# Copying every unit's V-product bank out in two column halves, on ScalarE and VectorE

## The chip, the cores and the metric

The kernel runs on one core of a Trainium2 chip. A core has a matrix engine (TensorE), three other compute engines (VectorE, ScalarE, GpSimd) and DMA queues that the sync engine and others feed. Every engine works through its own instructions in the order in which the program gives them, and waits on semaphores for the others. The metric is the device time of one execution, in microseconds; lower is better.

## The reference

The input x has 2048 rows (tokens) of 512 numbers. It is normalised by rows, and two branches are computed from it, attention with 32 heads of 16 numbers each and a gated MLP:

```
xn  = layernorm(x)
qkv = (xn @ wqkv)  -> q, k, v per head
p   = softmax(q @ k^T * 16 ** -0.5)
s   = (p @ v, heads side by side) @ wo
g   = silu(gelu(xn @ w1 + b1) @ w2 + b2)
out = x + s * g
```

All of it is in fp32. The attention is the part that the change touches.

## The kernel before, in words

The first part (to about 475 us) normalises x, makes q, k and v, runs the MLP and begins with the row maxima of the scores. The second part, the main loop of lines 954 to 972, is the attention, and the last part is the product with wo, the gate and the sum.

**Units and steps.** The attention is cut into 32 units: a group of 4 heads (8 groups) times a chunk of 512 queries (4 chunks). A unit `u` takes 16 steps, one for each block `k` of 128 keys; the loop's counter `n` is 16u + k. There are 512 steps and one more to finish.

**What a step does.** The string `ORDER[3]`, "TSXTTSTYV", gives the order of the work in a step for n from 2 to about 490:

- "T" (four times, `t_one`, line 702): one head's scores, keys along the partitions and 512 queries along the columns, as one product on TensorE (line 709) into a PSUM bank, and then the exponential of it by ScalarE (line 711) into a tile in SBUF. There are four banks for this, one (tile name `ps`) for the first T of a step and three (`pst`) in turn for the others. A T product waits until the exponential has read what was in its bank before.
- "S" (twice): scores of a later unit with queries along the partitions, as one product (line 178), and VectorE's maximum over the columns of it (line 184). They are needed for the softmax's shift.
- "X" and "Y": two half-wide products of the same kind in one bank, Y after X, and one maximum over both (line 184), recorded behind Y. So a step has three such reductions on VectorE.
- "V" (`pv_step`, line 768): the V product of the step before. Four matmuls on TensorE, one for each head, add `vsb` (the values, with a column of ones for the softmax's denominator) times the exponentials into one bank, the tile `pv`. The profile shows eight matmul records for it.

S, X and Y use three banks in a ring (`s_ring`): S takes the first and puts it at the end of the ring at once, X takes the next and Y puts that one back. By this order, the first S product of a step takes the bank of the first S of the step before, X takes that of the second S, and the second S takes that of X and Y. Each waits for VectorE's reduction of that bank.

In the last steps (n from about 491) there are no S, X and Y left; the order is "TTTTV", and the products with wo (line 880) run between.

**The end of a unit.** The pool `ps_v` has one bank, so the V products of all units go into the same one, one unit after the other. When the 16th V product of a unit is done (`k == NT - 1`), its result is copied from the bank to the tile `os` in SBUF (lines 777 to 784). The copy stands behind that V product in the program. ScalarE has the four exponentials of that step in front of it and those of the next step behind it; on VectorE, what stands in front of the place is the reduction of Y, and the next step's reductions follow. The first V product of the next unit comes at the end of the next step, after its T, S, X and Y products, and waits until the bank has been copied out.

For units 0 to 30 the whole copy is one instruction on ScalarE (line 781). For the last unit, 31, the columns are halved: ScalarE copies the first 256 (line 783), VectorE the other 256 (line 784).

From `os` the DMA queue then moves the denominators (line 794) and the four heads' rows (line 797) to other tiles. The moves are issued by the sync engine one step later; nine steps after the copy, VectorE takes the reciprocals of the denominators (line 802), which go through DRAM into a tile that GpSimd multiplies with (line 811).

**The loop's other work.** At some steps VectorE reduces a unit's maxima (line 239) or transposes them (line 258). In the last steps ScalarE and VectorE compute the gates (lines 834, 835) and VectorE multiplies the results (line 890).

Of the kernel before, what the change touches and what calls it, by code (L numbers as in the profile page):

```python
# [10 lines left out]
AF = mybir.ActivationFunctionType  # L11
# [29 lines left out]
HC = CH // 2  # L41
# [6 lines left out]
def fused(ctx: ExitStack, tc: tile.TileContext, x, wqk, wv, wo, w1, b1, w2, b2, out):  # L48
    nc = tc.nc
# [37 lines left out]
    NU = NG * NCH  # L87
# [679 lines left out]
    PV, OS, DN, DR = {}, {}, {}, {}  # L767
    def pv_step(u, k):
        g = u // NCH
        if k == 0:  # L770
            PV[u] = ps_v.tile([P, CH], F32, name="pv")
        for j in range(GH):
            h, w = (g * GH + j) * VW, VW if k else 32
            nc.tensor.matmul(PV[u][32 * j:32 * j + w, :], vsb[:, k, h:h + w], PT[u, k][:, j, :],  # L774
                             start=(k == 0), stop=(k == NT - 1))
        del PT[u, k]
        if k == NT - 1:
            OS[u] = wb.tile([P, CH], F32, name="os", bufs=1)
            pv = PV.pop(u)
            if u < NU - 1:  # L780
                nc.scalar.activation(OS[u], pv, AF.Copy)
            else:
                nc.scalar.activation(OS[u][:, :HC], pv[:, :HC], AF.Copy)
                nc.vector.tensor_copy(OS[u][:, HC:], pv[:, HC:])

    def o_rows(u, j):
        g, c = divmod(u, NCH)
# [166 lines left out]
    for n in range(L + 1):  # L954
        ua, ka = divmod(n, 16)
        want = due(n) - due(n - 1)
        i = 0
        for op in ORDER[want] if n > 1 else ("TTTTV", "TTSTSVT")[n]:
            if op in "SXY":
                s_op(op)  # L960
            elif op == "V":
                if n:
                    pv_step(*divmod(n - 1, 16))
                for _ in range(4):
                    tick()
                flush()
            else:
                if EARLY <= 4 * n + i < 4 * L:
                    t_one(ua, ka, i % 2, 1 - i // 2)
                for f, args in todo.get((n, i), []):  # L970
                    f(*args)
                i += 1
# [56 lines left out]
```

## Time and profile before

| what | value |
|---|---|
| runs, median of 3 | 1576.5 us (1576.18 to 1576.61) |
| the profiled execution's own time | 1576.49 us |
| its span, first to last instruction | 1574.7 us |
| granted TensorE clock | 1.000 |
| copies of line 781 | 31, 600 to 632 ns, from 510.6 to 1505.3 us |
| exponentials of line 711, 128 x 512 | 616 ns on the mean from banks `pst`, 606 from `ps` |
| maxima of line 184 | 686 ns on the mean, 2048 of them |

How to read it: the profile is one execution, and its times are microseconds from the start of the span unless they are marked as ns. PE is TensorE's matmuls, PEld its weight loads, DVE VectorE, ACT ScalarE, POOL GpSimd, SP the sync engine. L781 is line 781 of the kernel before. A row in order of time has the start, the duration, the engine, the line, the operation, the tile written and the tiles read, the shape and a count of merged instructions; in brackets stands idle time of the engine before it and what ended that. Matmuls are pipelined, and one that waits for its bank can show a longer time and not a gap. An ACT or DVE instruction can start before the end of the one in front of it.

### The profile page before, as it was taken

The page shows a single profiled execution, that of the slowest core. Times are in us where ns is not written, and L with a number is a line of the kernel's source. Part 1 is how long each engine was busy: PE and PEld are TensorE (multiplying, and loading weights), DVE is VectorE, ACT ScalarE, POOL GpSimd, SP SyncE. Part 2 cuts the span into 40 slices and gives each one's busy share as a digit, 9 for nine tenths or more (in the row PEclk, how much of TensorE's full clock was granted, in tenths as well). Part 3 has the DMA queues.
Part 4 walks back from the last instruction along what each step waited for, and adds up shares of the span by engine and source line. Part 5 has one row for each costly group of instructions (what it writes and reads, how often), then busy time and mean ns, then how long its engine had stood idle before and what let it go on. Part 6 is the DMA issues. An engine that isn't in the chain of part 4 may idle for free.

```text
span 1574.7 us, 32597 instructions
## 1 busy us (share of the span) xinstructions
PE 1563.7 (99%) x12234; PEld 954.6 (61%) x12234; DVE 1377.5 (87%) x2275; ACT 1254.2 (80%) x2516; POOL 378.0 (24%) x398
## 2 busy tenths in 40 slices
PE   9999999999999999999999999999999999999998
PEld 7899999999995444444444444444444444444455
DVE  7499999999998999999999999999999999999733
ACT  4333433434339999999999999999999999999994
POOL 4135575756741001001100200000010000000144
PEclk9999999999999999999999999999999999999999
DMA  6625443455422113111511411231041111110162
GB/s 208 151 60 142 129 139 98 130 151 131 132 84 76 42 31 71 31 36 35 86 31 32 69 36 37 49 53 29 22 79 30 33 29 31 42 29 23 45 214 96
DMA packets 79486, 116.92 MB, mean 74 GB/s; under 512 B 28868, under 2 KB 29124, under 8 KB 78152
## 3 DMA queue, kind: packets, MB, share of 16 engines
q1 hardware_dynamic: 75868, 102.42, 23.4%
q0 software_dynamic: 3264, 12.35, 4.0%
q8 instruction: 96, 1.57, 0.4%
q14 instruction: 62, 0.51, 0.1%
q10 hardware_dynamic: 196, 0.07, 0.0%
HBM read 84.35 MB, written 25.97 MB: 70 GB/s over the span
## 4 chain that ended last, share of the span: by engine, by line
PE 98%; DVE 1%; DMA 0%; issue 0%; ACT 0%; SPq 0%; POOL 0%; DVEq 0%; ACTq 0%
PE pv L774 32%; PE pst L709 16%; PE ps L709 14%; PE ps L560 13%; PE ps L178 9%; PE pst L560 7%; PE pv L560 2%; PE ps L79 2%; PE ps L880 1%; PE pst L79 1%; DVE slot L74 0%; DMA xt<-in_x 0%; DVE st L398 0%; DVE xn L412 0%; DVE slot L890 0%
## 5 line engine op out<-in xcount | busy, mean ns | idle before, releaser
L184 DVE TENSOR_REDUCE mx<-ps 128x2 f32<-128x512 f32 x2048 | 1299.6, 686 | 129.8 <-PE ps L178 49.1
L711 ACT ACTIVATE slot<-pst 128x512 f32<-128x512 f32 x1533 | 809.6, 616 | 2.1 <-PE ps L709 0.8
L774 PE MATMUL pv<-slot,vsb 128*17 128x512 f32 (+1 forms) x4096 | 539.2, 598 | 0.0
L178 PE MATMUL ps<-kt,slot 48*128 48x512 f32 x1364 | 383.7, 370 | 1.1 <-POOLq L216 1.1
L711 ACT ACTIVATE slot<-ps 128x512 f32<-128x512 f32 x515 | 311.7, 606 | 5.7 <-PE ps L709 3.6
L709 PE MATMUL pst<-qt,kt 50*128 50x512 f32 x1149 | 311.1, 406 | 0.5 <-DVE gt L642 0.3
L709 PEld LDWEIGHTS ps<-qt,kt 50*128 50x128 f32 x387 | 70.5, 183 | 323.8 <-ACT slot L711 322.9
L709 PEld LDWEIGHTS pst<-qt,kt 50*128 50x128 f32 x1149 | 211.6, 184 | 30.1 <-ACT slot L711 11.0
L178 PEld LDWEIGHTS ps<-kt,slot 48*128 48x128 f32 x1364 | 225.1, 184 | 3.1 <-POOLq L216 1.4
L560 PE MATMUL ps<-slot,w1h 64*128 64x512 f32 x1088 | 217.6, 394 | 0.0
L178 PE MATMUL ps<-kt,qz 48*128 48x512 f32 x512 | 212.8, 416 | 0.0
L709 PE MATMUL ps<-qt,kt 50*128 50x512 f32 x387 | 190.7, 495 | 0.0
L178 PE MATMUL ps<-slot,slot 48*128 48x512 f32 x598 | 167.8, 368 | 0.0
L560 PEld LDWEIGHTS ps<-slot,w1h 64*128 64x128 f32 x1088 | 150.4, 185 | 8.7 <-ACT junk L574 2.7
L560 PE MATMUL ps<-slot,w1l 64*128 64x512 f32 x544 | 141.0, 392 | 0.0
L358 POOL TENSOR_TENSOR hl<-hg,hh 128x512 fp32r<-128x512 f32 x76 | 96.7, 1294 | 135.9 <-ACT hh L357 87.7
L574 ACT ACTIVATE junk<-ident_r 1x1 f32<-1x1 f32 x92 | 18.0, 196 | 129.9 <-PE pst L560 125.4
L774 PEld LDWEIGHTS pv<-slot,vsb 128*17 128x17 f32 (+1 forms) x4096 | 68.8, 96 | 82.0 <-issue 26.7
L178 PEld LDWEIGHTS ps<-kt,qz 48*128 48x128 f32 x512 | 93.7, 183 | 15.9 <-DVE mx L184 0.6
L709 PE MATMUL pst<-qt,slot 50*128 50x512 f32 x384 | 102.3, 406 | 0.0
L178 PEld LDWEIGHTS ps<-slot,slot 48*128 48x128 f32 x598 | 98.7, 184 | 0.8
L242 POOL CAST nmh<-nm 128x16 fp32r<-128x16 f32 x32 | 6.3, 197 | 353.5 <-PE pst L709 176.4
(151 smaller groups left out, 1766.0 us busy)
## 6 DMA issues: line engine op xcount, KB each, us to landing
raw<-in_w SPq DMA_DIRECT2D x88, 256.0 KB
qk_h<-hh SPq DMA_DIRECT2D x32, 256.0 KB
qk_l<-hl SPq DMA_DIRECT2D x32, 256.0 KB
qt<-qk_h SPq DMA_DIRECT2D x128, 64.0 KB
slot<-qk_h SPq DMA_DIRECT2D x92, 64.0 KB
xt<-in_x SPq DMA_DIRECT2D x16, 256.0 KB
g_d<-gt POOLq DMA_DIRECT2D x16, 256.0 KB, 3.4
qt<-qk_l SPq DMA_DIRECT2D x64, 64.0 KB
```

The source lines that it names most:

```text
L79: nc.tensor.matmul(ps, lhs[a], rhs[b], start=first and n == 0, stop=last and n == 2)
L178: return nc.tensor.matmul(ps[:, c0:c0 + w], QS[u][r, p, qi * P:(qi + 1) * P], kts[u // NCH % KB][p][r, k0:k0 + w], start=True, stop=True).ins
L184: nc.vector.tensor_reduce(MX[u][:, 2 * p:2 * p + 2, qi, ki][:, heads, parts], ps.rearrange("p (n c) -> p n c", c=HC), axis=AX.X, op=OP.max)
L242: nc.gpsimd.tensor_copy(hl[:, 0], nm)
L358: nc.gpsimd.tensor_sub(hl, raw, hh.bitcast(F32))
L560: i = nc.tensor.matmul(ps, lhs[r], rhs[r], start=first, stop=last).ins
L574: i = nc.scalar.activation(junk[:, :1], ident_r[:1, :1].bitcast(F32), AF.Copy).ins
L709: nc.tensor.matmul(ps, kts[g % KB][p][r, k * P:(k + 1) * P], QT[u][r, p, :], start=True, stop=True)
L711: nc.scalar.activation(PT[u, k][:, 2 * p + a, :], ps, AF.Exp, scale=SCALE)
L774: nc.tensor.matmul(PV[u][32 * j:32 * j + w, :], vsb[:, k, h:h + w], PT[u, k][:, j, :], start=(k == 0), stop=(k == NT - 1))
L880: op = nc.tensor.matmul(PW[b][0], OTS[b, k][i][r], (wo_h, wo_l)[j][r, k], start=part == 0 and n == 0, stop=part == 3 and n == 5).ins
```

## The change

Every unit's result is copied as the last unit's was: columns 0 to 255 by ScalarE, columns 256 to 511 by VectorE, both recorded directly behind the unit's last V product. Nothing else is edited. On ScalarE, 31 instructions become half as wide. VectorE gets 31 new instructions, each between the reduction of Y in that step and the first reduction of the next step (for unit 30 behind a gate instruction of line 835). VectorE's copy waits for ScalarE's copy and for the earlier moves out of `os`, and the next unit's first V product, whose bank both copies read, comes behind both. The later lines move up by three: the two copies are lines 780 and 781 in the kernel after.

```diff
         if k == NT - 1:
             OS[u] = wb.tile([P, CH], F32, name="os", bufs=1)
             pv = PV.pop(u)
-            if u < NU - 1:
-                nc.scalar.activation(OS[u], pv, AF.Copy)
-            else:
-                nc.scalar.activation(OS[u][:, :HC], pv[:, :HC], AF.Copy)
-                nc.vector.tensor_copy(OS[u][:, HC:], pv[:, HC:])
+            nc.scalar.activation(OS[u][:, :HC], pv[:, :HC], AF.Copy)
+            nc.vector.tensor_copy(OS[u][:, HC:], pv[:, HC:])
```

## The prediction, made before the changed kernel ran

> **What bounds the kernel now.** I read the page first: the busy line, then the chain that ended last.
>
> ```profile
> PE 1563.7 (99%) x12234; PEld 954.6 (61%) x12234; DVE 1377.5 (87%) x2275; ACT 1254.2 (80%) x2516; POOL 378.0 (24%) x398
> ...
> PE 98%; DVE 1%; DMA 0%; issue 0%; ACT 0%; SPq 0%; POOL 0%; DVEq 0%; ACTq 0%
> PE pv L774 32%; PE pst L709 16%; PE ps L709 14%; PE ps L560 13%; PE ps L178 9%; PE pst L560 7%; PE pv L560 2%; PE ps L79 2%; PE ps L880 1%; PE pst L79 1%; DVE slot L74 0%; DMA xt<-in_x 0%; DVE st L398 0%; DVE xn L412 0%; DVE slot L890 0%
> ```
>
> The chain is TensorE, and neither copy line (781 or 784) is in it. But a busy PE hides short waits, since a product that waits for a bank is still shown as running. So I looked at the main loop's share of each engine:
>
> ```profile
> core 0: us, PE busy (x) PEld busy (x) DVE busy (x) ACT busy (x) POOL busy (x), PEclk, DMA share, GB/s
> 547.00:1460.00 913.00, 913.00 (x7100) 434.47 (x7093) 847.56 (x1401) 911.04 (x1802) 71.95 (x119) 1.00 0.19 41
> ```
>
> Of 913 us, ScalarE is busy for 911.0 and VectorE for 847.6 (93%): three engines run nearly level, and the slack on any of them is tenths of a microsecond per step. The next view is the order of time, TensorE alone, around one place where a unit ends. I call such a place a seam; a row "pv x8" is one step's V product.
>
> ```profile
> 805.73 1.05 PE L774 MATMUL pv<-slot,vsb 128*17 128x512 f32 x8
> ...
> 807.84 1.07 PE L774 MATMUL pv<-slot,vsb 128*32 128x512 f32 x8
> ...
> 810.22 1.05 PE L774 MATMUL pv<-slot,vsb 128*17 128x512 f32 x8
> ...
> 812.24 1.05 PE L774 MATMUL pv<-slot,vsb 128*17 128x512 f32 x8
> ...
> 814.28 1.05 PE L774 MATMUL pv<-slot,vsb 128*17 128x512 f32 x8
> ```
>
> V products of plain steps start 2.02 to 2.04 apart (810.22, 812.24, 814.28). The two steps at the seam take 2.11 (805.73 to 807.84) and 2.38 (to 810.22), 4.49 in place of 4.06. So today's copy costs 0.43 us per seam. The seams are alike; the chain in order of time has the same 2.39 and 2.38 elsewhere:
>
> ```profile
> 544.22 1.06 PE pv L774 x8
> 546.61 1.05 PE pv L774 x8
> ...
> 774.87 1.06 PE pv L774 x8
> 777.25 1.05 PE pv L774 x8
> ```
>
> Thirty seams (units 0 to 29) lie in the loop where a step has three S reductions, so all of today's price is about 30 x 0.43 = 12.9 us. No version of the copy can gain more than that.
>
> **Where the 0.43 sits.** The whole copy, and who waits for it:
>
> ```profile
> L781 ACTq EVENT_SEMAPHORE  x97: 17/38/475, 509.3 to 1504.4; - x97
> L781 ACT ACTIVATE os<-pv x31: 600/632/632, 510.6 to 1505.3; 128x512 f32<-128x512 f32 x31
> ...
>   PEld pv L774: 6.0, 30
> ```
>
> The new unit's first V product waits 6.0 / 30 = 0.2 us for the bank. The other part follows one step later. ScalarE at the seam:
>
> ```profile
> 807.15 0.63 ACT L781 ACTIVATE os<-pv 128x512 f32<-128x512 f32 x1
> 807.63 0.65 ACT L711 ACTIVATE slot<-ps 128x512 f32<-128x512 f32 x1
> 808.10 1.64 ACT L711 ACTIVATE slot<-pst 128x512 f32<-128x512 f32 x3
> 809.53 0.70 ACT L711 ACTIVATE slot<-ps 128x512 f32<-128x512 f32 x1
> ```
>
> Starts are 0.48 apart (807.15, 807.63, 808.10): the copy puts the queue back by 0.48. The last exponential of the three ends at 808.10 + 1.64 = 809.74, and the T product that wants its bank starts at 809.79, 0.49 long where an unhindered one takes 0.39:
>
> ```profile
> 808.83 0.49 PE L709 MATMUL ps<-qt,slot 50*128 50x512 f32 x1
> ...
> 809.17 0.39 PE L709 MATMUL pst<-qt,slot 50*128 50x512 f32 x1
> ...
> 809.40 0.41 PE L178 MATMUL ps<-kt,slot 48*128 48x512 f32 x1
> ...
> 809.79 0.49 PE L709 MATMUL pst<-qt,slot 50*128 50x512 f32 x1
> ```
>
> **What the change removes.** Half a copy from ScalarE. The last unit is already copied in halves, so both new instructions have a row:
>
> ```profile
> 1551.87 0.38 ACT L783 ACTIVATE os<-pv 128x256 f32<-128x256 f32 x1 [0.71 <-PE pv L774]
> ...
> 1552.29 0.42 DVE L784 COPY os<-pv 128x256 f32<-128x256 f32 x1 [1.00 <-ACT os L783]
> ```
>
> ScalarE's half takes 0.38 against 0.60 to 0.63, so every later exponential moves up by 0.22 to 0.25. That takes away the second part of today's price: the bank above would be free at about 809.5, ahead of its product.
>
> **What it adds.** The same two rows show the catch. VectorE's half does not run beside ScalarE's: it starts at 1552.29, 0.04 after the first half's end (1551.87 + 0.38 = 1552.25), and the profile names line 783 as what it waited for. Both read one bank, and the program orders them. So a parallel pair is not what is built. With the start of ScalarE's copy as zero (807.15 above), the bank comes free as follows: ScalarE's half ends at 0.42 (0.38, and 0.03 for a full queue, the difference of 632 and 600 ns above); VectorE's half runs from 0.46 to 0.88; the first V product follows 0.05 later (today 807.15 + 0.63 = 807.78, product at 807.84). That is 0.93, today 0.69: **0.24 later**, not earlier.
>
> **What is queued behind the wait on VectorE.** The copy stands behind the old step's last reduction and ahead of the new step's three. These are today's:
>
> ```profile
> 807.29 1.89 DVE L184 TENSOR_REDUCE mx<-ps 128x2 f32<-128x512 f32 x3
> 809.40 1.89 DVE L184 TENSOR_REDUCE mx<-ps 128x2 f32<-128x512 f32 x3 [0.22 <-PE ps L178]
> ```
>
> Three reductions of 0.69 in 1.89 start 0.60 apart, each beginning 0.09 before the one in front ends. Today they start at 0.14, 0.74 and 1.34; the third ends at 2.03. With the copy in front, the first starts at 0.46 + (0.42 - 0.09) = 0.79, the others at 1.39 and 1.99, and the third ends at 2.68: 0.65 later. Its bank goes, by the ring of three S banks, to the second S product of the following step, so that product waits, and the T, Y and V products queued behind it on TensorE wait too.
>
> No row shows this wait at a seam, but the trace has the same thing where the small reduction of line 239 slips into VectorE's queue:
>
> ```profile
> 830.65 0.27 DVE L239 TENSOR_REDUCE nm<-mx 128x16 f32<-128x128 f32 x1
> 830.84 1.28 DVE L184 TENSOR_REDUCE mx<-ps 128x2 f32<-128x512 f32 x2
> ```
>
> ```profile
> 830.51 1.05 PE L774 MATMUL pv<-slot,vsb 128*17 128x512 f32 x8
> ...
> 832.17 0.50 PE L178 MATMUL ps<-kt,slot 48*128 48x512 f32 x1
> ...
> 832.72 0.62 PE L774 MATMUL pv<-slot,vsb 128*17 128x512 f32 x4
> ```
>
> The reductions ran 0.19 late (830.65 to 830.84); the third ended at 830.84 + 1.28 = 832.12; the S product started 0.05 later and the V product 0.60 after that end; the step took 2.21, that is 0.18 longer. Nearly all of a lag on VectorE at this spot goes into the step.
>
> **The sum.** Next V product after the seam: 2.68 + 0.60 = 3.28. By TensorE alone it would be 0.93 + 2.03 = 2.96, so VectorE decides, by 0.32. Today it starts at 810.22 - 807.15 = 3.07. The price is **0.21 us** per seam. With ScalarE's half at the bare 0.38 everything behind it is 0.03 earlier: 0.18. I take 0.20. Does the lag go on? The delayed S product starts at 2.73; its reduction can begin at about 3.27 (0.50 and 0.04), the next at 3.87, ending at 4.56. The product that wants this bank stands 0.99 + 0.57 = 1.56 behind a V product (807.84 to the T product at 808.83, and from there to the second S product at 809.40), so at 4.84: no further loss. Then 30 x 0.20 = 6.0 us.
>
> Unit 30 ends in the stretch without S products:
>
> ```profile
> 1505.35 0.60 ACT L781 ACTIVATE os<-pv 128x512 f32<-128x512 f32 x1
> 1505.49 1.13 DVE L835 SCALAR_TENSOR_TENSOR gx<-slot,gx 128x512 f32<-128x512 f32 x1 [2.96 <-ACT slot L834]
> ...
> 1507.22 1.07 PE L774 MATMUL pv<-slot,vsb 128*32 128x512 f32 x8
> ```
>
> VectorE's half stands behind that gate, so it runs from about 1506.6 to 1507.0, and the V product begins at 1507.22 anyway. I cost it at nothing; the cover is 0.2 us, and without it unit 30 would add what a seam adds. Unit 31 is unchanged. The output moves on the DMA queue start some 0.25 later per unit, and their first reader is line 802's reciprocal, nine steps on. Sum: 1576.49 (span 1574.7 and 1.8 around it) + 6.0 = **1582.5 us**; the median of the runs is 1576.5, so no shift.
>
> Bounds of what no row shows. The start distance behind a PSUM copy: 0.33 as for reductions, at most its full 0.42 (+0.09 per seam). VectorE now passes four or five semaphores; on ScalarE such waits take 0.04 each (median above). They fall while VectorE waits anyway, so I take none; at most 0.15. Below: an ordinary S product may find 0.05 more slack than the 830 case. So 0.13 to 0.45 per seam, 3.9 to 13.5 us.
>
> The Trainium skill, "VectorE: DVE Perf Modes", section "The DRAIN you can't avoid", says that the next VectorE operation does not start until the pipe of the one before is empty. The 1.89 us rows disagree for reductions, which overlap by 0.09. If the rule held behind the copy, the sum would be 6.0 + 30 x 0.09 = 8.7 us, 1585.2.
>
> **The rivals.** (1) *Costlier hand-over.* The copy holds VectorE for its full 0.42 (0.10 of this rival's 0.18), or the semaphores are passed only after ScalarE's half: 0.30 to 0.45 per seam, 1585.5 to 1590. For it: five waits on one instruction. Against: VectorE is free from about -0.07, half a microsecond before it may start. (2) *The lag is absorbed.* If the second S product did not wait for VectorE, the next V product would come at 2.96, not 3.07: a gain of 0.11 per seam, 3.3 us, 1573.2. The point from which it decides: the third reduction ends by 2.36; between that and 2.47 some gain is left. For it: VectorE idles 0.22 ahead of 809.40, so part of a lag is taken up. Against it stands the 830 case, where 0.19 of lag cost 0.18. (3) *The halves overlap after all.* Then the bank is free at 0.47, TensorE is ready by 0.61 (805.73 + 2.03), the lag on VectorE is some 0.2, and nearly all of today's price goes: up to 12.9 us, 1564. Against it: the wait on line 783 in the row above.
>
> **How the numbers follow.** Forecast (0.13 to 0.30 per seam) 0.64; costlier hand-over 0.18; absorbed, wholly or in part, 0.15; overlap 0.03. What a measurement of this kernel can tell from no change is about 0.2%, 3.2 us. The forecast's lower edge (3.9) lies just above it, so 0.04 of its chance goes to "same", and 0.10 of the absorbed case; its other 0.05 and the overlap are "faster". Faster 0.08, same 0.14, slower 0.78. The range runs from 1578, below the forecast's lower edge of 1580.4, to 1588.5, inside the costlier case.
>
> **What would show it.** In the profile after: VectorE's copy with "ACT os" as its releaser, 30 times; the first V product waiting for VectorE; two equal seam steps of about 2.35 in place of 2.11 and 2.38; the reductions behind the copy without idle time; the second S product 0.5 long; no T product waiting for an exponential there; plain steps still 2.03. Wrong if the second seam step is near 2.03 (rival 2), or the first is under 2.05 (rival 3).

## The result, and the profile after

| | before | after |
|---|---|---|
| median of 5 runs | 1576.42 us (1576.18 to 1576.61) | 1582.38 us (1582.21 to 1582.53) |
| the profiled execution's own time | 1576.49 us | 1582.21 us |
| its span | 1574.7 us | 1580.4 us |
| granted TensorE clock | 1.000 | 1.000 |

The ratio is 1.0035, with a 95% interval of 1.0024 to 1.0046. The changed kernel is slower by 6.0 us; 1582.5 us was forecast.

The same seam as before, on TensorE in order of time. Now the first V product of the new unit shows what it waited for:

```profile
807.38 1.05 PE L774 MATMUL pv<-slot,vsb 128*17 128x512 f32 x8
...
809.73 1.07 PE L774 MATMUL pv<-slot,vsb 128*32 128x512 f32 x8 [0.24 <-DVE os L781]
...
811.19 0.39 PE L709 MATMUL pst<-qt,slot 50*128 50x512 f32 x1
811.52 0.50 PE L178 MATMUL ps<-kt,slot 48*128 48x512 f32 x1
811.53 0.49 PE L709 MATMUL pst<-qt,slot 50*128 50x512 f32 x1
...
812.07 1.05 PE L774 MATMUL pv<-slot,vsb 128*17 128x512 f32 x8
...
814.10 1.05 PE L774 MATMUL pv<-slot,vsb 128*17 128x512 f32 x8
```

The two steps at the seam now take 2.35 and 2.34 us (807.38, 809.73, 812.07), 4.69 in place of 4.49. The next one is a plain 2.03. So 0.20 us is lost at each of 30 seams, which is 6.0 us. The mean of all 30 seams went from 4.48 to 4.68 us, 5.9 us in all. The second S product of the following step, at 811.52, is 0.50 long: it waited. ScalarE and VectorE at the same place, in order of time:

```profile
808.80 0.42 ACT L780 ACTIVATE os<-pv 128x256 f32<-128x256 f32 x1
809.06 0.65 ACT L711 ACTIVATE slot<-ps 128x512 f32<-128x512 f32 x1
809.54 1.64 ACT L711 ACTIVATE slot<-pst 128x512 f32<-128x512 f32 x3
811.26 0.60 ACT L711 ACTIVATE slot<-ps 128x512 f32<-128x512 f32 x1
```

```profile
809.25 0.43 DVE L781 COPY os<-pv 128x256 f32<-128x256 f32 x1 [0.45 <-ACT os L780]
809.59 3.76 DVE L184 TENSOR_REDUCE mx<-ps 128x2 f32<-128x512 f32 x6
```

VectorE stood idle for 0.45 us until ScalarE's half was done (808.80 + 0.42 = 809.22), copied from 809.25, and then ran six reductions without a gap. The third of them starts at 809.59 + 2 x 0.60 and lasts 0.68, so it ends at 811.47; the S product follows 0.05 later and the V product 0.60 later. ScalarE did become lighter: its last exponential of the three ends at 809.54 + 1.64 = 811.18, ahead of the T product at 811.53 that wants the bank. The relief is real and comes to nothing, because by then VectorE is later than ScalarE used to be.

Who waited, over the whole execution, by the copy's line:

```profile
L781 DVEq EVENT_SEMAPHORE  x66: 21/50/50, 509.2 to 1511.3; - x66
L781 DVE COPY os<-pv x32: 410/424/426, 510.9 to 1558.0; 128x256 f32<-128x256 f32 x32
...
  ACT os L780: 14.5, 31
...
  PEld pv L774: 13.7, 31
```

VectorE waited 14.5 us for ScalarE's halves, 0.47 each, and TensorE's weight loads 13.7 us for VectorE's, where they had waited 6.0 for ScalarE's whole copy.

### The profile page after: what moved, and what is told of

Its sections match the earlier page's. It is cut to its first block, busy times and chain, and to the rows that moved or that the text cites. A ratio compares the mean times of both kernels' runs of the same rounds, so it can differ in the third digit from the quotient of the medians.

```text
span 1580.4 us, 32667 instructions
## 1 busy us (share of the span) xinstructions
PE 1561.9 (99%) x12234; PEld 957.7 (61%) x12234; DVE 1385.4 (88%) x2306; ACT 1250.9 (79%) x2516; POOL 378.6 (24%) x398
## 4 chain that ended last, share of the span: by engine, by line
PE 59%; ACT 37%; DVE 2%; issue 1%; DMA 0%; ACTq 0%; POOL 0%; SPq 0%; DVEq 0%
ACT slot L711 36%; PE pv L774 14%; PE ps L560 13%; PE ps L178 7%; PE pst L560 7%; PE ps L709 6%; PE pst L709 6%; PE pv L560 2%; PE ps L79 1%; PE ps L877 1%; PE pst L79 1%; DVE os L781 1%; ACT os L780 1%; DVE slot L74 0%; DMA xt<-in_x 0%
## 5 line engine op out<-in xcount | busy, mean ns | idle before, releaser
L709 PE MATMUL pst<-qt,kt 50*128 50x512 f32 x1149 | 307.9, 404 | 0.5 <-DVE gt L642 0.3
```

Of the source, the lines that this page charges most:

```text
L709: nc.tensor.matmul(ps, kts[g % KB][p][r, k * P:(k + 1) * P], QT[u][r, p, :], start=True, stop=True)
```

## The experiments

All of them edit the kernel before. Each is compared with runs of that kernel on the same chip: 1576.3 us for the lag of 768 numbers, the halves without the wait, VectorE's half first and the whole copy on VectorE, 1576.1 for the others, 1576.4 for the change itself. "Seam" is the two steps from the old unit's last V product to the new unit's second, as the mean of the 30 seams in the run's profile; before, it was 4.480 us.

| kernel | seam, mean of 30, us | 30 seams, against before, us | measured against before, us | ratio, 95% interval |
|---|---|---|---|---|
| the change | 4.677 | +5.9 | +6.0 | 1.0035 [1.0024, 1.0046] |
| lag on VectorE, 768 numbers | 4.659 | +5.4 | +5.3 | 1.0034 [1.0021, 1.0047] |
| lag, 384 numbers | 4.480 | 0.0 | +0.2 | 1.0000 [0.9991, 1.0009] |
| lag, 1024 numbers | 4.923 | +13.3 | +13.5 | 1.0087 [1.0072, 1.0102] |
| bank handed on late | 4.503 | +0.7 | +1.7 | 1.0013 [1.0003, 1.0022] |
| halves without the wait | 4.283 | -5.9 | -5.3 | 0.9967 [0.9954, 0.9979] |
| VectorE's half first | 4.594 | +3.4 | +3.8 | 1.0024 [1.0015, 1.0033] |
| both halves on ScalarE | 4.545 | +2.0 | +2.0 | 1.0014 [1.0004, 1.0023] |
| whole copy on VectorE | 4.399 | -2.4 | -2.6 | 0.9982 [0.9973, 0.9992] |

**The lag on VectorE alone.** ScalarE copies the whole bank as before, and VectorE gets something unrelated to do in the same place:

```diff
             if u < NU - 1:
                 nc.scalar.activation(OS[u], pv, AF.Copy)
+                lag = wb.tile([P, 1], F32, name="lag", bufs=1)
+                nc.vector.tensor_reduce(lag, vsb[:, 0:2, 0:384], axis=AX.XY, op=OP.max)
```

> ScalarE copies the whole bank as before, and VectorE runs an unrelated maximum over 768 numbers of the resident values, which waits for nothing, in the place where the changed kernel has its copy (31 times, units 0 to 30). It holds VectorE for about 768/512 x 0.53 + 0.07 = 0.87 us from -0.07, so the next reductions start near 0.80, as in the changed kernel (0.79), while the bank comes free as early as before. Theory (VectorE's lag sets the next V product): the first V product stays at 0.69, the second is at about 3.28, +0.21 us per seam, 1582.7 us. Rival (the late bank is what costs): no change, 1576.5 us. Rival (each adds its own share): half of it, about 1579.5 us.

Measured: 1581.6 us. VectorE and then TensorE at a seam, in order of time:

```profile
808.16 0.94 DVE L783 TENSOR_REDUCE lag<-vsb 128x1 f32<-128x768 f32 x1
809.01 3.16 DVE L184 TENSOR_REDUCE mx<-ps 128x2 f32<-128x512 f32 x5
```

```profile
806.83 1.05 PE L774 MATMUL pv<-slot,vsb 128*17 128x512 f32 x8
808.93 1.07 PE L774 MATMUL pv<-slot,vsb 128*32 128x512 f32 x8
811.50 1.05 PE L774 MATMUL pv<-slot,vsb 128*17 128x512 f32 x8
```

The first V product is as early as before (a step of 2.10), and all the loss is in the second step, 2.57. The third reduction ends at 809.01 + 1.20 + 0.68 = 810.89, and the V product comes 0.61 behind it. So VectorE's lag alone, without a late bank, costs nearly what the change costs.

**Less and more of it.** The same edit with 384 and with 1024 numbers (`vsb[:, 0:1, 0:384]` and `vsb[:, 0:2, 0:512]`).

> The unrelated maximum on VectorE again, over 384 numbers: about 0.46 us of VectorE. Theory (VectorE's lag costs only beyond the point where ScalarE's queue already holds the step): the reductions behind start at 0.38, the third ends at 2.27, the V product by that would be at 2.87, below the 3.07 that ScalarE's queue sets: no change, 1576.4 us. Rival (every piece of work added to VectorE costs its share): half of the 768 case, +2.6 us, 1579 us.

> The same over 1024 numbers: about 1.13 us of VectorE. Theory (beyond the break-even each further 0.1 us of lag costs 0.1 us): the reductions behind start at 1.04, 0.27 later than with 768, so the second V product comes 0.27 later, +0.45 us per seam over before, 1576.4 + 13.5 = 1590 us. Rival (one of the next steps takes part of it up): +8 to 10 us.

Measured: 1576.28 and 1589.66 us. VectorE at a seam with 384 numbers:

```profile
807.11 0.54 DVE L783 TENSOR_REDUCE lag<-vsb 128x1 f32<-128x384 f32 x1
807.57 2.57 DVE L184 TENSOR_REDUCE mx<-ps 128x2 f32<-128x512 f32 x4
```

TensorE's V products at a seam, first with 384, then with 1024:

```profile
805.78 1.05 PE L774 MATMUL pv<-slot,vsb 128*17 128x512 f32 x8
807.88 1.07 PE L774 MATMUL pv<-slot,vsb 128*32 128x512 f32 x8
810.26 1.05 PE L774 MATMUL pv<-slot,vsb 128*17 128x512 f32 x8
```

```profile
809.02 1.05 PE L774 MATMUL pv<-slot,vsb 128*17 128x512 f32 x8
811.10 1.06 PE L774 MATMUL pv<-slot,vsb 128*32 128x512 f32 x8
813.93 1.05 PE L774 MATMUL pv<-slot,vsb 128*17 128x512 f32 x8
```

A small lag costs nothing (2.10 and 2.38, as before), since ScalarE's queue already holds the step for that long. From start to start, the work with 384 numbers holds VectorE for 0.46 us (807.11 to 807.57), that with 768 for 0.85 (808.16 to 809.01) and that with 1024 for 1.13. From 768 to 1024 numbers the mean seam grows by 0.26 us for these 0.28. The cost begins at a point and is then paid nearly in full.

**The late bank alone.** ScalarE copies the whole bank; the first V product waits, besides, for a small GpSimd copy behind ScalarE's.

```diff
+            if 0 < u < NU - 1:
+                late = wb.tile([P, 16], F32, name="late", bufs=1)
+                tok = nc.gpsimd.tensor_copy(late, LAST[0][:, :16]).ins
...
+            if 0 < u < NU - 1 and k == 0 and j == 0:
+                tc.add_manual_dep(op, tok.name, SYNC, reason="bank late")
```

> ScalarE copies the whole bank as before and VectorE gets nothing; the first V product of units 1 to 30 waits, besides, for a small GpSimd copy (128 x 16) that itself waits for ScalarE's copy. So the bank is handed on about 0.2 to 0.3 us later, at about 0.95, as late as in the changed kernel, without any lag on VectorE. Theory (the late bank hides behind ScalarE's queue): by TensorE alone the second V product would be at 0.95 + 2.03 = 2.98, below the 3.07 of before: no change, 1576.4 us, at most +1. Rival (the late bank is paid in full): +0.25 us for each of 30 seams, 1584 us.

Measured: 1577.85 us, somewhat above what was expected. Two seams of this kernel on TensorE, an ordinary one and one of the worst:

```profile
808.82 1.05 PE L778 MATMUL pv<-slot,vsb 128*17 128x512 f32 x8
811.16 1.06 PE L778 MATMUL pv<-slot,vsb 128*32 128x512 f32 x8 [0.25 <-POOL late L775]
813.29 1.05 PE L778 MATMUL pv<-slot,vsb 128*17 128x512 f32 x8
```

```profile
610.30 1.05 PE L778 MATMUL pv<-slot,vsb 128*17 128x512 f32 x8
613.27 1.06 PE L778 MATMUL pv<-slot,vsb 128*32 128x512 f32 x8 [0.88 <-POOL late L775]
615.30 1.05 PE L778 MATMUL pv<-slot,vsb 128*17 128x512 f32 x8
```

At the ordinary seam the bank came as late as in the changed kernel (a step of 2.34 against 2.35), and the following step was only 2.13: the sum is 4.47, nothing lost. At the other one the GpSimd copy itself came late, the first step took 2.97, and the sum is 5.00. Taken over the 16 steps of a unit, 22 of the 30 seams cost nothing (each within 0.03 us of before). The first and this one cost 0.18 and 0.72, and six others, every fourth one from 743 us on, 0.08 to 0.18 each, in the step behind the seam. Together that is 1.65 us, about what the runs show (+1.7); why the step behind every fourth seam is longer was not traced. The profiled execution is the slowest of the ten (1579.99 us); 2.0 us of that lies ahead of the first V product. The rival, 0.25 us at every seam, is out.

**The two halves without the wait.** ScalarE's half reads the resident values in place of the bank, so that VectorE's half has nothing to wait for. Columns 0 to 255 of the results of units 0 to 30 are thereby left out; the kernel serves the timing alone:

```diff
             if u < NU - 1:
-                nc.scalar.activation(OS[u], pv, AF.Copy)
+                nc.scalar.activation(OS[u][:, :HC], vsb[:, 0, :HC], AF.Copy)
+                nc.vector.tensor_copy(OS[u][:, HC:], pv[:, HC:])
```

> ScalarE's half reads the resident values and not the bank, so columns 0 to 255 of the first 31 units' results are wrong, but its width and place are those of the changed kernel; VectorE's half no longer has to wait for it. Theory (the wait of one half for the other is the whole loss): VectorE copies from -0.07 to 0.35, its reductions run only 0.12 late, the third ends at 2.15; ScalarE's queue then decides: its third exponential ends at 2.38 in place of 2.59 and the second V product follows at 2.85 in place of 3.07, -0.22 us per seam, 1570 us. Rival (the added work on VectorE costs, wait or not): not below 1576.5 us, up to 1582.

Measured: 1570.98 us. VectorE, ScalarE and TensorE's V products at a seam:

```profile
805.38 0.41 DVE L782 COPY os<-pv 128x256 f32<-128x256 f32 x1
805.71 3.83 DVE L184 TENSOR_REDUCE mx<-ps 128x2 f32<-128x512 f32 x6
```

```profile
805.46 0.44 ACT L781 ACTIVATE os<-vsb 128x256 f32<-128x256 f32 x1
805.77 0.62 ACT L711 ACTIVATE slot<-ps 128x512 f32<-128x512 f32 x1
806.25 1.61 ACT L711 ACTIVATE slot<-pst 128x512 f32<-128x512 f32 x3
```

```profile
804.05 1.05 PE L774 MATMUL pv<-slot,vsb 128*17 128x512 f32 x8
...
806.09 1.06 PE L774 MATMUL pv<-slot,vsb 128*32 128x512 f32 x8
...
808.34 1.05 PE L774 MATMUL pv<-slot,vsb 128*17 128x512 f32 x8
```

VectorE's copy starts at once and beside ScalarE's. Instructions of the same widths in the same places make the kernel 5.3 us faster than before without the wait, and 6.0 slower with it. The difference, 11 us, is the price of the wait. ScalarE's half has another source here (0.44 us long against 0.42); no run shows both engines reading one bank at the same time.

**The other order.** VectorE's columns first, ScalarE's behind them.

```diff
             if u < NU - 1:
-                nc.scalar.activation(OS[u], pv, AF.Copy)
+                nc.vector.tensor_copy(OS[u][:, HC:], pv[:, HC:])
+                nc.scalar.activation(OS[u][:, :HC], pv[:, :HC], AF.Copy)
```

> The two halves in the other order: VectorE's columns first, ScalarE's behind them. Theory: VectorE copies from -0.07 to 0.35 and its reductions run only 0.12 late; ScalarE stands still until 0.39, copies to 0.78, and the first V product comes at 0.83; ScalarE's third exponential ends at about 2.71 in place of 2.59, so the lateness moves to ScalarE and the second V product comes at about 3.19: +0.12 us per seam, 1580 us, with a T product waiting for an exponential again. Rival (the sum of both halves on the bank decides, whoever is first): as the changed kernel, 1582.4 us. Rival (only VectorE's lag matters): below before, about 1573.

Measured: 1580.1 us. ScalarE at a seam:

```profile
808.35 0.38 ACT L782 ACTIVATE os<-pv 128x256 f32<-128x256 f32 x1 [0.22 <-DVE os L781]
808.63 0.59 ACT L711 ACTIVATE slot<-ps 128x512 f32<-128x512 f32 x1
809.11 1.58 ACT L711 ACTIVATE slot<-pst 128x512 f32<-128x512 f32 x3
```

Now ScalarE stands idle, and its exponentials are late instead of VectorE's reductions: on the mean of the 30 seams the fourth ends 4.12 us behind the start of the old unit's last V product, 0.12 later than before (4.00). Whoever goes second pays.

**Both halves on ScalarE.** In place of the whole copy, two instructions of half the width, both on ScalarE.

> Both halves on ScalarE, one behind the other, for units 0 to 30; nothing on VectorE. Theory (the loss comes from the wait of one engine for the other, not from halving): the second half ends at 0.69, the first V product of the new unit comes at 0.74 (0.69 before), the exponentials behind are 0.06 later, and so is the second V product: +0.06 us per seam, 1578.2 us. Rival (two narrow copies of one bank are what costs): as the changed kernel, 1582.4 us.

Measured: 1578.16 us. Halving itself is cheap: at a seam near 806 us the two halves hold ScalarE for 0.53 us from start to start (807.46 to 807.99), where the whole copy held it for 0.48 (807.15 to 807.63), and the mean seam is 0.06 us longer.

**The whole copy on VectorE.** No part on ScalarE, for units 0 to 30:

```diff
             if u < NU - 1:
-                nc.scalar.activation(OS[u], pv, AF.Copy)
+                nc.vector.tensor_copy(OS[u], pv)
```

> The whole copy on VectorE for units 0 to 30, none on ScalarE. Theory: it starts at -0.07 and ends at 0.62, so the bank is free as before (0.69); the reductions run 0.39 late, the third ends at 2.42 and the second V product comes at 3.02 in place of 3.07: -0.05 us per seam, 1575 us, about no change. Rival (work added to VectorE is what costs): twice the columns of the changed kernel, so at least its +6 us, 1582 or more.

Measured: 1573.68 us, the fastest of the kernels that copy the whole bank, and 0.18% below the kernel before. VectorE and TensorE at a seam:

```profile
806.02 0.68 DVE L781 COPY os<-pv 128x512 f32<-128x512 f32 x1
806.62 3.76 DVE L184 TENSOR_REDUCE mx<-ps 128x2 f32<-128x512 f32 x6
```

```profile
804.71 1.05 PE L774 MATMUL pv<-slot,vsb 128*17 128x512 f32 x8
...
806.76 1.06 PE L774 MATMUL pv<-slot,vsb 128*32 128x512 f32 x8
...
809.10 1.05 PE L774 MATMUL pv<-slot,vsb 128*17 128x512 f32 x8
```

Twice the columns on VectorE, and yet 8.7 us less than the change: the copy begins as soon as VectorE is free and waits for no other engine's half. The third reduction ends at 806.62 + 1.20 + 0.68 = 808.50, the V product is 0.60 behind it. So this version, too, is held by VectorE at the seam, by 0.31 us (its second step takes 2.34, a plain one 2.03).

**Two distances for all of them.** In the change, the lags of 768 and 1024 numbers and the whole copy on VectorE, the new unit's second V product starts 0.59 to 0.63 us behind the end of the third reduction, at each of the 30 seams. In the kernel before, with the lag of 384 numbers, without the wait, with VectorE's half first and with both halves on ScalarE, it starts 0.47 to 0.49 behind the end of the fourth exponential behind the copy, at each seam; the late bank does so at 28 of 30, and at the two seams where the GpSimd copy came latest a plain step of 2.03 us follows. So otherwise either VectorE or ScalarE holds the product, whichever is later with its distance. Before, ScalarE held it at 4.00 + 0.48 = 4.48 us behind the old unit's last V product, and the third reduction ended at 3.44. By this estimate it could have ended at 4.48 - 0.60 = 3.88, which is 0.44 later, without a cost. With 384 numbers it ended 0.22 later and nothing was lost, in the changed kernel 0.64 later, which leaves the 0.20 that was paid.

## Why the prediction was right

*What bounds the seam.* Right, and shown from both sides: the unrelated maximum brings the loss without a late bank, the late bank alone does not at an ordinary seam, and the V product stands 0.60 behind the third reduction's end in the changed kernel, with the lag of 768 numbers and with the whole copy on VectorE.

*ScalarE's half, hand-over, VectorE's half.* Forecast with ScalarE's start as zero: 0.42, 0.46, 0.88, and the first V product at 0.93. Measured, with 808.80 as zero: 0.42, 0.45, 0.88, 0.93.

*The lag.* Forecast: reductions from 0.79, the third ending at 2.68, the V product at 3.28. Measured: 0.79, 2.67, 3.27. The price of 0.20 us per seam was met.

*No further loss.* Right: the step after the seam is 2.03 long.

*Costed at nothing.* This was right for unit 30, in the stretch without S products: VectorE's copy runs behind the gate as forecast, and the V product begins 1.87 us after ScalarE's copy (1512.95 less 1511.08), as before (1507.22 less 1505.35). VectorE and TensorE there:

```profile
1511.22 1.13 DVE L832 SCALAR_TENSOR_TENSOR gx<-slot,gx 128x512 f32<-128x512 f32 x1 [2.96 <-ACT slot L831]
1512.27 0.41 DVE L781 COPY os<-pv 128x256 f32<-128x256 f32 x1
```

```profile
1512.95 1.06 PE L774 MATMUL pv<-slot,vsb 128*32 128x512 f32 x8
```

*The semaphores.* There are two to a copy (66 for 32 copies) and not the four or five of the prediction. They take 0.05 us each on VectorE, but the copy starts 0.03 after ScalarE's half ends, so they lie under the wait, as assumed.

*The rule on the empty pipe.* The section of the Trainium skill that the prediction names ("VectorE: DVE Perf Modes", "The DRAIN you can't avoid") also has an exception, that an operation which is not held starts earlier; the prediction gave the rule without it. Behind the copy, too, the next reduction starts before the copy ends: 809.25 + 0.43 = 809.68, the reduction at 809.59. The 0.09 of the row was the right value, and the unconditional rule's 1585.2 us was 2.8 too much.

*The exponentials.* Who ended TensorE's idle time at line 709, in the kernel before and in the one after:

```profile
  ACT slot L711: 446.5, 569
```

```profile
  ACT slot L711: 431.9, 509
```

Sixty waits for an exponential are gone, two for each seam, as forecast. The count does not show that ScalarE's relief took them away: with the lag of 768 numbers, where ScalarE copies the whole bank, it is 509 too, because TensorE comes late to these products. The relief is in ScalarE's own rows: the fourth exponential ends 3.79 us behind the old unit's last V product in place of 4.00 (means of 30 seams), 0.21 earlier; 0.22 to 0.25 was forecast.

*What was not right* is what that relief is worth. The prediction says that it takes away the whole second part of today's price, and prices the overlap case at up to 12.9 us of gain, all of today's cost. The kernel without the wait gains 5.3 us: its second step at the seam is still 2.25 long (806.09 to 808.34). ScalarE's half copy still puts the exponentials back; the last ends at 806.25 + 1.61 = 807.86, and the V product follows 0.48 behind, the distance at which ScalarE held it before (809.74, 810.22). The forecast did not rest on this, since VectorE was later. Of the experiments, the whole copy on VectorE was forecast to gain 1.5 us (1575) and gained 2.6: the copy starts 1.31 us behind the old unit's last V product (804.71, 806.02), where 1.35 was reckoned (1.42 to ScalarE's copy, less 0.07).

## What to carry to other kernels

Two halves of one PSUM bank on two engines aren't run side by side when the program orders them; the second engine then pays with a standstill in the middle of its queue, and what it has queued behind is what counts. Before an engine with 93% load is given a wait, look for what its next outputs release: here the third instruction behind the copy set the time, not the copy. Slack has a threshold: work that held VectorE for 0.46 us at the seam cost nothing, and 0.85 us cost 5 us in all.

## What the runs showed of the hardware that was not expected

The chain of waits that ended last changed far more than the time. It was 98% TensorE before; after, by engine:

```profile
PE 59%; ACT 37%; DVE 2%; issue 1%; DMA 0%; ACTq 0%; POOL 0%; SPq 0%; DVEq 0%
```

With a time that differs by 0.35%, and plain steps of 2.03 us in both, this is no sign of a new bound. Among the experiments the shares do not follow what holds the seam either: the lag of 768 numbers, held by VectorE like the changed kernel, has 98% TensorE and 0% ScalarE, and both halves on ScalarE has 57% and 40%. Where TensorE and ScalarE run nearly level, the chain seems to follow either of them. The seams had to be read from the order of time.
